# Window attention on one core: the right-hand columns of windows laid end to end over five blocks, a last block of three lines, and a start whose clearing moves to GpSimd

## The chip, the cores and the metric

The kernel runs on one core of one Trainium2 chip. The metric is the time of one execution in microseconds on the device. Times below are from three runs of the kernel before and from one profiled execution of it.

## The reference, cut to what matters

The image x is 511 x 511 with 192 channels in bf16 (73 x 73 windows of 7 x 7 pixels). A 3 x 3 depthwise convolution is added to it, the sum is normalised over its channels, each window does attention over its own 49 pixels with 4 heads of 48, and a projection is added back.

```python
xp = jnp.pad(x, ((0, 0), (1, 1), (1, 1), (0, 0)))
for i in range(3):
    for j in range(3):
        pe = pe + xp[:, i:i + H, j:j + W, :] * dw_pe[i, j][None, None, None, :]
x0 = x + pe
h = _layernorm(x0, axis=-1)
# h into windows of 7 x 7: 73 * 73 windows of 49 pixels
qkv = (hw @ w_qkv).reshape(-1, 49, 3, 4, 48)
attn = softmax(einsum('wnhd,wmhd->whnm', q, k) * 48 ** -0.5)
out = einsum('whnm,wmhd->wnhd', attn, v).reshape(-1, 49, 192) @ w_o
return x0 + out          # out back from windows to the image
```

## The kernel before

The 5329 windows are cut into 42 blocks of up to 128 windows; a window is a partition. `_blocks` gives each block as lines `(a, b, da, db, n, p)`: n windows from window (a, b) on, along a row (`db` = 1) or down a column (`da` = 1), on partitions from p. The first 64 windows of each of the 73 rows are lines of 64, two to a block. The nine columns on the right (columns 64 to 72) are lines of 64 down, rows 1 to 64. Blocks 0 to 35 are pairs of rows; block 36 is the last row and column 64; blocks 37 to 40 are pairs of columns; what is left in the right-hand corners, 81 windows, is block 41, nine lines of nine.

A block needs two loads. `load_xp` fetches XP, the patches for the convolution: 9 x 9 pixels on 81 partitions, then windows, then channels. One transfer brings, for one line, one of the nine pixel columns of the patch (9 patch rows x n windows x 192 channels); where a patch leaves the image, `clear` copies zeros. `load_x` fetches X, the pixels by windows (128 x 49 x 192); the same tile later takes the convolution, then the projection, and is stored from there. XP has one buffer, X has three. Loads and stores go through SP's queue in the order in which they are written; a few XP loads go through ScalarE's queue.

The main loop goes over 667 groups of 8 windows; a block has 16 groups (slots 0 to 15), the last one 11. While block b is in attention (`stage_A`: q and k, `stage_V`, `stage_B`: scores and their exponential, `stage_D`: the product with v, `stage_E`: transposition into HO), the same loop carries, spread over the slots by `part`,

- the projection of block b-1 in 13 pieces (`proj`): ScalarE copies a piece out of PSUM to pO and GpSimd adds it to X; with `direct` VectorE adds it from PSUM; then the stores of block b-1 in four chunks of rows (`store`),
- the convolution of block b+1: 192 matmuls, one per channel (`conv_mm`, L318), each ten of them added to X by VectorE (L324); then its layer norm: statistics (L329), `rstd` on GpSimd (L338, L339), the product h (L344), and its transposition into HO (`ln_tr`, L354 and L364),
- the loads of block b+2: XP once the convolution of block b+1 has read the one XP buffer, X once block b-1 is stored. For a block with 14 loads of X (two lines) an earlier path issues them as the stores of block b-1 leave.

Ahead of the loop block 0 is convolved and normalised with nothing beside it (`Next.prepare`), after some tiles have been cleared (HO, k, pt, v).

Of the kernel before, what the change touches and what calls it, by code (L numbers as in the profile page):

```python
# [32 lines left out]
WS, NH, C, DH, S = 7, 4, 192, 48, 49  # L33
BLK, CH, KP, KT = 128, 8, 81, 96
# [4 lines left out]
_HALF = 64  # L39


def _blocks(nwr, nwc):

    full, tall = min(_HALF, nwc), min(_HALF, nwr)
    top = min(1, nwr - tall)
    halves = [(a, 0, 0, 1, full) for a in range(nwr)]
    halves += [(top, b, 1, 0, tall) for b in range(full, nwc)]
    blocks = [[h + (64 * i,) for i, h in enumerate(halves[k : k + 2])] for k in range(0, len(halves), 2)]
    if nwc > full:
        cur, p = (blocks.pop(), 64) if len(halves) % 2 else ([], 0)  # L50
        for a in [*range(top), *range(top + tall, nwr)]:
            n = nwc - full
            if p + n > BLK:
                blocks.append(cur)
                cur, p = [], 0
            cur.append((a, full, 0, 1, n, p))
            p += n
        if cur:
            blocks.append(cur)
    return blocks  # L60


class _Kernel:
# [140 lines left out]
    def load_xp(self, b):  # L204

        nc, x, XP, XPr, W, NWR, NWC = self.nc, self.x, self.XP, self.XPr, self.W, self.NWR, self.NWC
        blocks, clear, dram = _blocks(NWR, NWC), self.clear, self.dram
        for a0, b0, da, db, n, p0 in blocks[b]:
            left = [0] if b0 == 0 else []
            right = [] if b0 + (n - 1) * db < NWC - 1 else list(range(n)) if da else [n - 1]  # L210
            if left and (b == 0 or any(ln[1] for bb in blocks[:b] for ln in bb)):
                yield clear(XPr[0], p0, n if da else 1)
            if right:
                yield clear(XPr[8], p0 + right[0], len(right))
            last = a0 + (n - 1) * da
            cuts = [0] + ([1] if da and a0 == 0 else []) + ([n - 1] if da and last == NWR - 1 else []) + [n]
            for i, j in zip(cuts, cuts[1:]):
                if j <= i:
                    continue
                top, bot = a0 + i * da == 0, a0 + (j - 1) * da == NWR - 1  # L220
                if top:
                    yield clear(XP[0:9], p0 + i, j - i)
                if bot:
                    yield clear(XP[KP - 9 : KP], p0 + i, j - i)
                pr0, pr1 = (1 if top else 0), (8 if bot else 9)
                for pc in range(9):
                    q, sh = (WS - 1, -1) if pc == 0 else (0, 1) if pc == 8 else (pc - 1, 0)
                    n0, n1 = i, j
                    if pc == 0 and left:
                        n0 = j if da else i + 1  # L230
                    if pc == 8 and right:
                        n1 = i if da else j - 1
                    if n1 <= n0:
                        continue
                    dims = [[W * C, pr1 - pr0], [WS * C * (W * da + db), n1 - n0], [1, C]]
                    dst = XPr[pc, pr0:pr1, p0 + n0 : p0 + n1, :]
                    src = dram(x, WS * (a0 + n0 * da) - 1 + pr0, WS * (b0 + n0 * db + sh) + q, dims)
                    q = nc.scalar if (len(blocks[b]) > 2 and pc % 3 == 2) or (b == 0 and pc % 2) else nc.sync
                    yield lambda q=q, dst=dst, src=src: q.dma_start(out=dst, in_=src)  # L239

    def strips(self, b, r0, r1):

        W = self.W
        for a0, b0, da, db, n, p0 in _blocks(self.NWR, self.NWC)[b]:
            yield slice(p0, p0 + n), (WS * a0 + r0, WS * b0, [[WS * C * (W * da + db), n], [W * C, r1 - r0], [1, WS * C]])

    def load_x(self, b):

        nc = self.nc
        short = len(_blocks(self.NWR, self.NWC)[b]) > 2  # L250
        for r0, r1 in [(0, WS)] if short else [(r, r + 1) for r in range(WS)]:
            for p, at in self.strips(b, r0, r1):
                dst = self.X[b % 3][p, r0 * WS : r1 * WS, :].rearrange("p (r q) c -> p r (q c)", q=WS)
                q = nc.sync
                yield lambda q=q, dst=dst, src=self.dram(self.x, *at): q.dma_start(out=dst, in_=src)


    def fast(self, ctx):
        nc, tc = self.nc, self.tc
# [12 lines left out]
        o_ = pool.tile([128, 2, 2, C], BF, name="o")  # L272
        pO = _Rot([pool.tile([128, 4, C], BF, name=f"pO{i}") for i in range(2)])
        r_ = pool.tile([128, 16], F32, name="rs")
        nc.vector.memset(HO[0][:], 0.0)
        nc.gpsimd.memset(HO[1][:], 0.0)
        nc.vector.memset(k_[:], 0.0)
        for t in [pt] + vv:
            nc.vector.memset(t[:], 1.0)

        x, out, W = self.x, self.out, self.W
        NWR, NWC = self.NWR, self.NWC
# [1 line left out]
        NB = len(blocks)  # L284
# [42 lines left out]
        def ln_stat(b, i):  # L327
            s = min(2 * i, S - 2)
            nc.vector.bn_stats(  # L329
                out=bnst[:, s : s + 2, :].rearrange("p a f -> p (a f)"),  # L330
                in_=self.X[b % 3][:, s : s + 2, :].rearrange("p s c -> p c s"),
            )

        def ln_rstd(r):

            t = slice(r * WS, (r + 1) * WS)
            e = nc.gpsimd
            e.tensor_scalar(out=rstd[:, t], in0=bnst[:, t, 2], scalar1=1.0 / C, scalar2=self.eps, op0=ALU.mult, op1=ALU.add)  # L338
            e.tensor_tensor(out=rstd[:, t], in0=rstd[:, t], in1=expo[:].to_broadcast([128, WS]), op=ALU.pow)  # L339

        def ln_norm(b, r, eng):
            t = slice(r * WS, (r + 1) * WS)
            h = self.X[2][:, t, :] if b == 0 else hr.next()
            eng.tensor_tensor(  # L344
                out=h[:, :, :], in0=self.X[b % 3][:, t, :], in1=rstd[:, t].unsqueeze(2).to_broadcast([128, WS, C]), op=ALU.mult
            )
            return h
# [151 lines left out]
        class Next:  # L499
# [15 lines left out]

            def prepare(n_):

                while n_.si < STATS:
                    ln_stat(n_.b, n_.si)
                    n_.si += 1  # L520
                for r in range(WS):
                    ln_rstd(r)
                    n_.ready.append((now[0], ln_norm(n_.b, r, nc.gpsimd if r < 2 else nc.vector)))
                    if r >= 2:
                        ln_tr(n_.b, n_.tr, n_.ready[n_.tr][1])
                        n_.tr += 1

# [24 lines left out]
            t()  # L552
        n.prepare()
        n.finish()
        sq = []
        nn = None

# [3 lines left out]
        for g in range(NG + LE + 1):  # L561
# [18 lines left out]
            def part(lo, hi, total, at=None):  # L580
                return min(total, max(0, int(((f if at is None else at) - lo) / (hi - lo) * total + 0.5)))

            pj = []
            even = b < NB and nslot >= 14
            if 1 <= b and ck >= (LE - 1 if even else LE):
                goal = 13 if b == NB else min(13, 3 * ck - 2) if even else part(0.10, 0.48, 13)
                while pdone < goal:
# [20 lines left out]
            def hook(share):  # L608

                nonlocal xpn, xln  # L610
                at = f0 + (f - f0) * share
                if n and n.conv.c == C:
                    n.stats(int(s_start + (s_goal - s_start) * share))
                while sq and sq[0][0] <= g + share:
                    _, bb, k = sq.pop(0)
                    store(bb, k)
                    stored[bb] = k + 1
                    freed[k] = g + share
                if even and 1 <= b and len(xl) == 2 * WS:
                    while xln < len(xl) and freed.get(xln // 4, NG) + 0.9 <= g + share:  # L620
                        xl[xln]()
                        xln += 1
                if n is None or n.conv.c == C:
                    goal = part(0.38 + d, 0.96 if many else 0.58 + 0.5 * d, len(xp), at)
                    while xpn < goal:
                        xp[xpn]()
                        xpn += 1
                    if b < 1 or stored.get(b - 1, 0) == len(CHUNKS):
                        goal = part(0.5, 0.7, len(xl), at)
                        while xln < goal:  # L630
                            xl[xln]()
                            xln += 1
# [5 lines left out]
            def project(groups_):  # L638
                nonlocal sdone
                for s0 in groups_:  # L640
                    proj(b - 1, s0, b == NB and s0 % 8 == 0)
                    while sdone < len(CHUNKS) and CHUNKS[sdone][1] * WS <= min(S, s0 + 4):
                        sq.append((g + 0.9, b - 1, sdone))
                        sdone += 1
# [286 lines left out]
```

## Time and profile before

| what | value |
|---|---|
| runs of the kernel | 3611.0, 3615.5 and 3599.74 us, median 3611.0 us |
| the profiled execution | 3608.29 us, of which the span of instructions is 3606.6 us |
| mean granted clock of TensorE | 0.986 |
| busy: PE, PEld, DVE, ACT, POOL | 92%, 82%, 69%, 78%, 57% |

The span is what the trace shows; 1.7 us lie around it. The busy shares are means over the whole span, in which one block takes some 82 us, so what a stage costs has to be read in stretches of a block. A stretch is best cut where the first matmul of a convolution stands, since the convolution of a block and the load of XP for the one after it follow each other in one buffer.

### The profile page before, as it was taken

Reading aid. Unit: us, or ns where it says so; the run is one execution under the profiler, and the core shown is the slowest. Engines: PE = TensorE matmul, PEld = TensorE weight load, DVE = VectorE, ACT = ScalarE, POOL = GpSimd, SP = SyncE. Lnnn points to the kernel's source line nnn. Section 1 sums busy time; section 2 is a strip of 40 time slices with the busy share of each in tenths; the row PEclk is TensorE's granted clock in tenths of the full one; section 3 lists DMA queues with packets and bytes.
Section 4 is the critical chain, followed back from the end, with each engine's and each line's share of the span. In section 5 each row is a group of like instructions: output and inputs, shape, how many; then the busy total and the mean of one; then the engine's idle time right before and its main releaser. Section 6 shows DMA issues by size and latency. Waiting matters only on the chain.

```text
span 3606.6 us, 170088 instructions
## 1 busy us (share of the span) xinstructions
PE 3330.4 (92%) x77393; PEld 2941.1 (82%) x77393; DVE 2504.5 (69%) x4236; ACT 2804.7 (78%) x3512; POOL 2063.1 (57%) x1425
## 2 busy tenths in 40 slices
PE   4999999999999999999999999999999999999687
PEld 3888888888888888888888888888888888888575
DVE  6767667777776667777777766777777766666563
ACT  1788888888888888888888888888888877777575
POOL 4356655666555566566655566656665555555453
PEclk9999999999999999999999999999999998999898
DMA  6344444444434444444444444444444444444311
GB/s 145 74 101 108 115 117 116 117 113 113 103 101 101 106 112 116 119 118 114 115 104 101 101 107 112 116 117 118 114 117 103 101 101 101 101 101 105 67 32 46
DMA packets 529123, 377.39 MB, mean 105 GB/s; under 512 B 453595, under 2 KB 453787, under 8 KB 528393
## 3 DMA queue, kind: packets, MB, share of 16 engines
q1 hardware_dynamic: 521440, 363.75, 40.8%
q8 instruction: 607, 9.95, 1.2%
q10 hardware_dynamic: 6953, 2.69, 0.4%
q14 instruction: 123, 1.01, 0.1%
HBM read 265.31 MB, written 100.27 MB: 101 GB/s over the span
## 4 chain that ended last, share of the span: by engine, by line
PE 63%; DVE 15%; ACT 9%; issue 4%; POOL 3%; SPq 3%; DMA 3%; ACTq 0%; POOLq 0%; DVEq 0%
PE ps L378 19%; PE ps L473 11%; PE psc L318 9%; PE ps L394 9%; PE ps L461 7%; DVE bnst L329 6%; DVE o L447 4%; PE psc L354 4%; ACT pO L484 4%; ACT v L402 3%; SPq L239 3%; PE ps L437 2%; POOL h L344 2%; DVE HO L462 2%; PE ps L416 2%
## 5 line engine op out<-in xcount | busy, mean ns | idle before, releaser
L488 POOL TENSOR_TENSOR X<-X,pO 128x768 bf16<-128x768 bf16 (+1 forms) x539 | 845.8, 1573 | 1097.9 <-ACT pO L484 1095.5
L378 PE MATMUL ps<-HO,Wqk 96*128 96x196 bf16 (+1 forms) x7680 | 1318.4, 283 | 89.3 <-ACT pO L484 49.0
L318 PEld LDWEIGHTS <-XP 81*128 81x128 bf16 x8064 | 1014.4, 175 | 105.3 <-issue 95.5
L318 PE MATMUL psc<-T,XP 81*128 81x49 bf16 x8064 | 1036.0, 205 | 48.6 <-DMA XP<-in_x_dram 34.6
L378 PEld LDWEIGHTS <-Wqk 96*128 96x128 bf16 x7680 | 753.7, 104 | 150.6 <-issue 22.5
L324 DVE TENSOR_TENSOR X<-psc,X 128x490 bf16<-128x490 f32 x840 | 539.1, 645 | 448.9 <-PE psc L318 445.9
L386 ACT CAST k<-ps 128x784 bf16<-128x784 f32 x667 | 542.0, 813 | 243.3 <-PE ps L378 220.2
L344 POOL TENSOR_TENSOR h<-X,rstd 128x1344 bf16<-128x1344 bf16 x287 | 697.9, 2432 | 22.5
L386 ACT CAST q<-ps 128x784 bf16<-128x784 f32 x667 | 542.2, 813 | 187.2 <-PE ps L378 146.5
L394 PE MATMUL ps<-Wv,HO 96*128 96x192 bf16 x5336 | 646.6, 245 | 22.8 <-ACT q L386 19.7
L447 DVE TENSOR_TENSOR o<-ps,rs 128x768 bf16<-128x768 f32 x667 | 638.8, 958 | 23.3
L394 PEld LDWEIGHTS <-HO 96*128 96x128 bf16 x5336 | 515.0, 104 | 106.6 <-issue 69.7
L424 ACT ACTIVATE pt<-ps 128x784 bf16<-128x784 f32 x667 | 550.1, 825 | 55.8 <-PE ps L416 40.5
L402 ACT CAST v<-ps 128x768 bf16<-128x768 f32 x667 | 536.3, 804 | 69.3 <-PE ps L394 58.6
L329 DVE BATCH_NORM_STATS2 bnst<-X 128x6 f32<-128x384 bf16 x1050 | 533.9, 547 | 4.2
L462 DVE COPY HO<-ps 96x784 bf16<-96x784 bf16 x667 | 380.0, 570 | 209.5 <-PE ps L461 207.4
L484 ACT CAST pO<-ps 128x768 bf16<-128x768 f32 x498 | 397.7, 799 | 145.8 <-PE ps L473 127.5
L473 PE MATMUL ps<-Wo,HO 96*128 96x192 bf16 x4116 | 491.3, 262 | 1.4 <-DVE HO L462 0.7
L461 PEld LDWEIGHTS <-o 128*96 128x96 bf16 x5336 | 364.8, 125 | 109.3 <-DVE o L447 78.5
L339 POOL TENSOR_TENSOR rstd<-rstd,expo 128x7 f32<-128x7 f32 x294 | 439.2, 1494 | 24.5
L461 PE MATMUL ps<-ident,o 128*96 128x128 bf16 x5336 | 421.4, 222 | 24.8 <-DVE o L447 22.6
L473 PEld LDWEIGHTS <-HO 96*128 96x128 bf16 x4116 | 436.8, 186 | 1.9 <-DVE HO L462 0.9
(55 smaller groups left out, 2604.9 us busy)
## 6 DMA issues: line engine op xcount, KB each, us to landing
XP<-in_x_dram SPq DMA_DIRECT2D x644, 216.0 KB
X<-in_x_dram SPq DMA_DIRECT2D x574, 168.0 KB
out_dram<-X SPq DMA_DIRECT2D x246, 336.0 KB
XP<-in_x_dram SPq DMA_DIRECT2D x71, 212.6 KB
out_dram<-X SPq DMA_DIRECT2D x82, 168.0 KB
XP<-in_x_dram SPq DMA_DIRECT2D x12, 192.0 KB
X<-in_x_dram SPq DMA_DIRECT2D x9, 165.4 KB
XP<-in_x_dram SPq DMA_DIRECT2D x42, 30.4 KB
```

Of the source, the lines that this page charges most:

```text
L318: mm(cv.ps[:, (c % 10) * S : (c % 10 + 1) * S], lhsT=XP[0:KP, :, c], rhs=T[0:KP, c, :], start=True, stop=True)
L329: nc.vector.bn_stats(out=bnst[:, s : s + 2, :].rearrange("p a f -> p (a f)"), in_=self.X[b % 3][:, s : s + 2, :].rearrange("p s c -> p c s"),)
L344: eng.tensor_tensor(out=h[:, :, :], in0=self.X[b % 3][:, t, :], in1=rstd[:, t].unsqueeze(2).to_broadcast([128, WS, C]), op=ALU.mult)
L378: mm(ps[:, ab * 512 + i * m * S : ab * 512 + (i + 1) * m * S], lhsT=self.Wqk[kt][0:KT, which * 2 + ab, :], rhs=HO[b % 2][0:KT, kt, ck * CH ...
L386: nc.scalar.copy(out=dst[:, :, 0:TOK], in_=two_bank(ps, TOK))
L394: mm(ps[:, col : col + C], lhsT=HO[b % 2][0:KT, kt, w : w + 2, :].rearrange("p w s -> p (w s)"), rhs=self.Wv[kt][0:KT, :], start=(kt == 0) ...
L402: eng(out=v_[:].rearrange("p (b j) h e -> p b (j h) e", b=2)[:, :, :, 0:DH], in_=two_bank(ps, 2 * C).rearrange("p b (g d) -> p b g d", d=DH),)
L424: nc.scalar.activation(out=pt[:, 0 : 16 * S].rearrange("p (b n) -> p b n", b=2), in_=two_bank(ps, 8 * S), func=ACTF.Exp, scale=SCALE)
L447: nc.vector.tensor_tensor(out=o_[:].rearrange("p b q (h d) -> p b (q h) d", d=DH), in0=ov[:, :, :, 0:DH], in1=r_[:].rearrange("p (b g) -> ...
L461: mm(ev, lhsT=o_[:, sl, Q, kt * KT : (kt + 1) * KT], rhs=ident[:], start=True, stop=True, is_transpose=True)
L473: mm(ps[:, col : col + C], lhsT=HO[b % 2][0:KT, kt, :, s0 + i], rhs=self.Wo[kt][0:KT, :], start=(kt == 0), stop=(kt == 1))
L488: nc.gpsimd.tensor_tensor(out=xv, in0=xv, in1=o[:, 0:n, :], op=ALU.add)
```

## The change

The right-hand columns: `_blocks` now takes the nine columns with rows 1 to 71 and lays them end to end, cutting wherever a block is full. 639 windows fill blocks 36 to 40 (2, 3, 3, 3 and 2 lines, the last with 127 windows). Block 41 is the last row (64 windows) and the nine corner windows of the first and of the last row: three lines, 82 windows. The number of blocks and groups stays.

With that: `load_x` fetches X of a line with all seven pixel rows in one transfer wherever a block has columns; `strips` cuts a line of n windows at the last multiple of 16, for loads and stores alike, so a line of 71 becomes 64 and 7; ScalarE's queue issues XP loads for block 0 alone; XP loads of blocks of three lines are written by 0.62 of a block instead of 0.96.

The start: HO[0], k, pt and v are cleared on GpSimd instead of VectorE, and HO[1] on GpSimd after block 0 is prepared; `prepare` takes the rows one by one (statistics, rstd, h of the row before on VectorE or GpSimd in turn, transposition), where all 25 statistics came first.

The last block: the projection of block 40 stands in slots 1 to 5 of block 41 (1, 3, 3, 3, 3 pieces) instead of slots 2 to 5 (6, 3, 3, 1), and every second piece of it is added by VectorE.

```diff
-    full, tall = min(_HALF, nwc), min(_HALF, nwr)
-    top = min(1, nwr - tall)
+    full = min(_HALF, nwc)
+    n = nwc - full
     halves = [(a, 0, 0, 1, full) for a in range(nwr)]
-    halves += [(top, b, 1, 0, tall) for b in range(full, nwc)]
...
+    if n:
+        last, p = (blocks.pop(), _HALF) if nwr % 2 else ([], 0)
+        cur, q = [], 0
+        for b in range(full, nwc):
+            a = 1
+            while a < nwr - 1:
+                m = min(nwr - 1 - a, BLK - q)
+                cur.append((a, b, 1, 0, m, q))
+                a, q = a + m, q + m
+                if q == BLK:
+                    blocks.append(cur)
+                    cur, q = [], 0
         if cur:
             blocks.append(cur)
+        blocks.append(last + [(a, full, 0, 1, n, p + i * n) for i, a in enumerate((0, nwr - 1))])
...
-                    q = nc.scalar if (len(blocks[b]) > 2 and pc % 3 == 2) or (b == 0 and pc % 2) else nc.sync
+                    q = nc.scalar if b == 0 and pc % 2 else nc.sync
...
+            for i, m in ((0, n - n % 16), (n - n % 16, n % 16)):
+                if m:
+                    at = (WS * (a0 + i * da) + r0, WS * (b0 + i * db), [[WS * C * (W * da + db), m], [W * C, r1 - r0], [1, WS * C]])
+                    yield slice(p0 + i, p0 + i + m), at
...
-        short = len(_blocks(self.NWR, self.NWC)[b]) > 2
+        lines = _blocks(self.NWR, self.NWC)[b]
+        short = len(lines) > 2 or any(ln[2] for ln in lines)
...
-        nc.vector.memset(HO[0][:], 0.0)
-        nc.gpsimd.memset(HO[1][:], 0.0)
-        nc.vector.memset(k_[:], 0.0)
+        nc.gpsimd.memset(HO[0][:], 0.0)
+        nc.gpsimd.memset(k_[:], 0.0)
         for t in [pt] + vv:
-            nc.vector.memset(t[:], 1.0)
+            nc.gpsimd.memset(t[:], 1.0)
...
-                while n_.si < STATS:
-                    ln_stat(n_.b, n_.si)
-                    n_.si += 1
-                for r in range(WS):
-                    ln_rstd(r)
-                    n_.ready.append((now[0], ln_norm(n_.b, r, nc.gpsimd if r < 2 else nc.vector)))
-                    if r >= 2:
+                for r in range(WS + 1):
+                    if r < WS:
+                        while n_.si < min(STATS, ((r + 1) * WS + 1) // 2):
+                            ln_stat(n_.b, n_.si)
+                            n_.si += 1
+                        ln_rstd(r)
+                    if r:
+                        n_.ready.append((now[0], ln_norm(n_.b, r - 1, nc.vector if r % 2 else nc.gpsimd)))
+                    if r > 1:
...
         n.finish()
+        nc.gpsimd.memset(HO[1][:], 0.0)
...
-            even = b < NB and nslot >= 14
+            even = b < NB and nslot >= 8
...
-                    goal = part(0.38 + d, 0.96 if many else 0.58 + 0.5 * d, len(xp), at)
+                    goal = part(0.38 + d, 0.62 if many else 0.58 + 0.5 * d, len(xp), at)
...
-                    proj(b - 1, s0, b == NB and s0 % 8 == 0)
+                    proj(b - 1, s0, b >= NB - 1 and s0 % 8 == 0)
```

The first place is SP's queue while block 35 is in attention: the stores of block 34 and the loads of block 37, which is made of columns. Before (`out_dram` is the output, X_74 the X buffer, `in_x_dram` the image; shapes are partitions first):

```order
L303 DMA out_dram<-X_74 64x2x1344 x4
L255 DMA X_74<-in_x_dram 64x1344 x8
L303 DMA out_dram<-X_74 64x2x1344 x2
L303 DMA out_dram<-X_74 64x1344 x2
L255 DMA X_74<-in_x_dram 64x1344 x6
L239 DMA XP<-in_x_dram 9x64x192 x18
```

The same place in the change:

```order
L310 DMA out_dram<-X_74 64x2x1344 x6
L310 DMA out_dram<-X_74 64x1344 x2
L243 DMA XP<-in_x_dram 9x14x192 x9
L243 DMA XP<-in_x_dram 9x71x192 x5
L263 DMA X_74<-in_x_dram 14x7x1344
L243 DMA XP<-in_x_dram 9x71x192 x4
L263 DMA X_74<-in_x_dram 64x7x1344
L243 DMA XP<-in_x_dram 9x43x192 x7
L263 DMA X_74<-in_x_dram 7x7x1344
L243 DMA XP<-in_x_dram 9x43x192 x2
L263 DMA X_74<-in_x_dram 32x7x1344
L263 DMA X_74<-in_x_dram 11x7x1344
```

X was fetched ahead of XP in 14 transfers; it is now fetched in five, which stand among the 27 of XP and behind them. In every block of columns it is so.

The second place is SP's queue while block 39 is in attention, with the loads of block 41. Before, this is the beginning of 74 transfers on SP (27 more are on ScalarE's queue):

```order
L200 DMA XP<-T 9x192
L200 DMA XP<-T 9x9x192
L239 DMA XP<-in_x_dram 8x9x192 x6
L200 DMA XP<-T 9x192
L239 DMA XP<-in_x_dram 9x9x192 x2
L255 DMA X_75<-in_x_dram 9x7x1344
L239 DMA XP<-in_x_dram 9x9x192 x2
L255 DMA X_75<-in_x_dram 9x7x1344
```

The same place in the change, from the first transfer (`XP<-T` is `clear`) to the clears ahead of the third line:

```order
L204 DMA XP<-T 9x192
L204 DMA XP<-T 9x64x192
L243 DMA XP<-in_x_dram 8x63x192
L243 DMA XP<-in_x_dram 8x64x192 x8
L204 DMA XP<-T 9x192
L204 DMA XP<-T 9x9x192
L243 DMA XP<-in_x_dram 8x9x192 x6
L263 DMA X_75<-in_x_dram 64x7x1344
L243 DMA XP<-in_x_dram 8x9x192 x2
L243 DMA XP<-in_x_dram 8x8x192
L204 DMA XP<-T 9x192
L204 DMA XP<-T 9x9x192
```

All of block 41's patches are now three lines: nine transfers of a row of 64 windows, eighteen small ones and six clears, where there were 81 small ones and eleven clears.

The third place is VectorE at the start, from the branch into the fast path on. Before, the rows of clearing and the first two additions of the convolution of block 0:

```order
L267 MEMSET expo 128x1
L275 MEMSET HO_260 128x8192
L277 MEMSET k 128x408
L279 MEMSET pt 128x800
L279 MEMSET v_268 128x784
L279 MEMSET v_269 128x784
L324 TENSOR_TENSOR X_73<-psc_67,X_73 128x49x10
L324 TENSOR_TENSOR X_73<-psc_68,X_73 128x49x10
```

In the change the additions come at once, and behind the last of them the statistics, h (X_75) and the transposed rows (HO) alternate (the last rows of that stretch):

```order
L275 MEMSET expo 128x1
L331 TENSOR_TENSOR X_73<-psc_67,X_73 128x49x10
...
L336 BN_STATS bnst<-X_73 128x6 x7
L351 TENSOR_TENSOR X_75<-X_73,rstd 128x1344
L336 BN_STATS bnst<-X_73 128x6 x4
L371 COPY HO_260<-psc_67 96x128x7
L351 TENSOR_TENSOR X_75<-X_73,rstd 128x1344
```

The five clears are gone from VectorE's queue, and four products h stand between the statistics instead of five behind them.

## Rows read from the trace of the kernel before

**Rows 1.** The page: span, engines, and the granted clock in 40 slices.

```profile
span 3606.6 us, 170088 instructions
...
PE 3330.4 (92%) x77393; PEld 2941.1 (82%) x77393; DVE 2504.5 (69%) x4236; ACT 2804.7 (78%) x3512; POOL 2063.1 (57%) x1425
...
PEclk9999999999999999999999999999999998999898
```

**Rows 2.** Busy time by stretch, cut where each next convolution starts (blocks 33 to 39).

```profile
2793.50:2875.20 81.70, 78.25 (x1854) 69.21 (x1853) 58.81 (x101) 66.95 (x85) 49.08 (x34) 1.00 0.44 111
2875.20:2962.80 87.60, 82.13 (x1930) 71.68 (x1929) 60.51 (x103) 69.67 (x88) 49.11 (x34) 0.98 0.43 103
2962.80:3048.80 86.00, 79.72 (x1861) 70.33 (x1862) 59.68 (x101) 67.55 (x85) 48.98 (x34) 0.98 0.44 106
3048.80:3139.40 90.60, 84.62 (x1861) 75.15 (x1862) 59.16 (x100) 67.25 (x84) 49.04 (x34) 0.91 0.42 100
3139.40:3224.70 85.30, 78.09 (x1860) 69.00 (x1861) 59.18 (x100) 67.11 (x84) 49.00 (x34) 1.00 0.44 106
3224.70:3312.70 88.00, 81.82 (x1861) 72.72 (x1861) 59.10 (x100) 67.26 (x84) 48.98 (x34) 0.94 0.43 103
3312.70:3433.90 121.20, 81.00 (x1861) 71.14 (x1862) 59.20 (x100) 67.68 (x84) 49.06 (x34) 0.85 0.28 56
```

**Rows 3.** The convolution's matmuls alone (L318), from first to last, blocks 34 to 38.

```profile
2875.20:2920.00 44.80, 24.46 (x192) 23.90 (x191) 1.00 0.32 81
2962.80:3008.30 45.50, 24.57 (x192) 24.07 (x192) 1.00 0.39 101
3048.80:3100.20 51.40, 28.25 (x192) 26.41 (x192) 0.83 0.33 86
3139.40:3184.90 45.50, 24.59 (x192) 24.07 (x192) 1.00 0.39 101
3224.70:3273.80 49.10, 27.01 (x192) 25.59 (x192) 0.90 0.36 91
```

**Rows 4.** Waits of PE from 3359 to 3440 us: sum, times, longest.

```profile
PE psc L318 <- DMA XP<-in_x_dram: 33.0, 1, 33.0
```

**Rows 5.** Transfers into XP, 3359 to 3440 us: ns of an issue (min/median/max), first and last.

```profile
L239 SPq DMA_DIRECT2D XP<-in_x_dram x54: 676/763/803, 3364.0 to 3431.6; - x54
L239 ACTq DMA_DIRECT2D XP<-in_x_dram x27: 686/783/1441, 3359.8 to 3396.7; - x27
L200 SPq DMA_DIRECT2D XP<-T x11: 757/777/857, 3359.6 to 3427.1; - x11
```

**Rows 6.** SP's queue in order of time: loads of a block of rows, then of columns.

```profile
2838.27 3.10 SPq L239 DMA_DIRECT2D XP<-in_x_dram  x3
2841.49 5.16 SPq L255 DMA_DIRECT2D X<-in_x_dram  x6
2846.69 21.04 SPq L239 DMA_DIRECT2D XP<-in_x_dram  x15
...
3100.68 34.55 SPq L239 DMA_DIRECT2D XP<-in_x_dram  x18
```

**Rows 7.** The start: VectorE's timeline, waits for X of L324, GpSimd's rstd.

```profile
36.12 6.88 DVE L275 MEMSET HO<- 128x8192 uint32 x1 [1.68 <-issue]
...
45.84 1.18 DVE L324 TENSOR_TENSOR X<-psc,X 128x490 bf16<-128x490 f32 x2
...
L324 DVEq EVENT_SEMAPHORE  x4: 49/50/50, 40.4 to 42.0; - x4
...
L339 POOL TENSOR_TENSOR rstd<-rstd,expo 128x7 f32<-128x7 f32 x7 | 15.1, 2155 | 0.6
```

**Rows 8.** The end: one stretch of block 41, last additions on GpSimd, last stores.

```profile
3524.20:3559.80 35.60, 32.10 (x626) 25.94 (x626) 10.82 (x19) 27.71 (x38) 19.88 (x13) 0.95 0.28 70
...
3589.68 4.88 POOL L488 TENSOR_TENSOR X<-X,pO 128x768 bf16<-128x768 bf16 x3
...
3587.75 16.39 SPq L303 DMA_DIRECT2D out_dram<-X  x36
```

More of the change, by code (lines that the diff above doesn't have):

```diff
@@ L42, in _blocks @@
 def _blocks(nwr, nwc):
-    full, tall = min(_HALF, nwc), min(_HALF, nwr)
-    top = min(1, nwr - tall)
+    full = min(_HALF, nwc)
+    n = nwc - full
+    assert 2 * n <= _HALF
     halves = [(a, 0, 0, 1, full) for a in range(nwr)]
-    halves += [(top, b, 1, 0, tall) for b in range(full, nwc)]
     blocks = [[h + (64 * i,) for i, h in enumerate(halves[k : k + 2])] for k in range(0, len(halves), 2)]
[L49 to L57, printed above, removed]
+    if n:
[10 more added lines that the diff above has]
+                    cur, q = [], 0
         if cur:
             blocks.append(cur)
+        blocks.append(last + [(a, full, 0, 1, n, p + i * n) for i, a in enumerate((0, nwr - 1))])
     return blocks
@@ L244, in strips @@
         for a0, b0, da, db, n, p0 in _blocks(self.NWR, self.NWC)[b]:
-            yield slice(p0, p0 + n), (WS * a0 + r0, WS * b0, [[WS * C * (W * da + db), n], [W * C, r1 - r0], [1, WS * C]])
+            for i, m in ((0, n - n % 16), (n - n % 16, n % 16)):
+                if m:
+                    at = (WS * (a0 + i * da) + r0, WS * (b0 + i * db), [[WS * C * (W * da + db), m], [W * C, r1 - r0], [1, WS * C]])
+                    yield slice(p0 + i, p0 + i + m), at
     def load_x(self, b):
         nc = self.nc
-        short = len(_blocks(self.NWR, self.NWC)[b]) > 2
+        lines = _blocks(self.NWR, self.NWC)[b]
+        short = len(lines) > 2 or any(ln[2] for ln in lines)
         for r0, r1 in [(0, WS)] if short else [(r, r + 1) for r in range(WS)]:
```

## Prediction, written before the changed kernel ran

> **What bounds the kernel now.** The page first [rows 1]: TensorE (PE) is busy 92% of a span of 3606.6 us, and its granted clock is full (2.4 GHz) until the last sixth of the slices (a 9 is 0.9 or more). So for most of the span PE sets the pace, and nothing that only takes work off another engine moves the end. Then the stretches cut at each convolution's start [rows 2]. A block of rows takes 81.7 us. Block 34, during which the first columns are loaded, takes 87.6, and blocks 35 to 38 take 86.0, 90.6, 85.3 and 88.0; block 39 takes 121.2 with PE busy for 81.0 of it. Three places are thus worth looking at: blocks 34 to 38, block 39, and the two ends, where no block overlaps another.
>
> Block 39 is plain: PE waits once, 33.0 us, for XP [rows 4]. The convolution of block 41 is waiting for its patches. Behind that wait stand 92 transfers into XP, 65 of them on SP at some 0.76 us each, issued from 3359.6 to 3431.6 us [rows 5]. Issuing is the bound, 72 us of it, since one transfer brings nine windows only. With PE idle the clock falls to half, 1.2 GHz, and the stretch has 0.85 of the full one [rows 2].
>
> Blocks 34 to 38 are subtler. XP has one buffer, so a block is a loop: the convolution (45 us at full clock, up to 51.4 at a mean of 0.83 [rows 3]), then the loads, then the next convolution. A block of rows has its 18 XP loads and six X loads issued in 3.10 + 5.16 + 21.04 us, 1.40 us for an XP load [rows 6]. For columns 18 XP loads alone take 34.55 us, 1.92 each [rows 6]: the same bytes, spread over more of the image. In block 36 the first is issued at 3100.68 us, 0.5 us behind the convolution, the last is through at 3135.23, and the next convolution starts at 3139.4, 4.2 us later [rows 2, 3, 6]. From the first issue that is 38.7 us. So the loop takes 45.5 + 0.5 + 38.7 = 84.7 us at full clock, just what PE itself needs for such a block (85.3 [rows 2]). PE waits there hardly at all, but nothing is left either: each microsecond that the loads grow by is paid.
>
> **The change, part by part.**
>
> *Start.* VectorE (DVE) spends 36.12 to 45.8 us on clears before its first addition, and PE waits for that [rows 7]. Without them the addition waits for X alone, whose last semaphore is there at 42.0 us [rows 7]: 45.8 - 42.0 = 3.8 us gained (2.8 to 5.4: the four waits ended between 40.4 and 42.0, and one landing may lie later by 1 us). The clears move to GpSimd, which has no work until the first rstd, well past 60 us; HO[1] then lies on it beside the first slots of block 0, where it has none either. If that cover were gone, its 13 us would stand on the path. Preparing block 0 row by row starts rstd and the products h among the statistics, but rstd stays a chain of seven on GpSimd, 15.1 us at a mean of 2.16 [rows 7], and GpSimd now has three products h instead of two. I count 1.2 us gained (0 to 3). Together **-5** (-2 to -8).
>
> *Columns end to end.* The windows in XP are as many as before, so I take 38.7 us from first issue to restart, and add what is new among the loads.
> X: it left ahead of XP, now it stands among it. The six X loads of a row block put 29.3 - 18 x 1.40 = 4.1 us between its XP loads [rows 6], 0.7 us for 64 window rows of pixels. Written ahead of the last XP load are, in blocks 34 to 38, 64, 85, 92, 106 and 56 windows of seven pixel rows, which is 7.0, 9.3, 10.1, 11.6 and 6.1 such loads: 4.9 + 6.5 + 7.0 + 8.1 + 4.3 = 30.8 us. That is the upper bound; nothing is the lower, if X runs in the gaps that XP leaves (a column's XP moves at 1.40/1.92 of the rate of a row's).
> Short pieces: nine XP loads of 14 windows cost 9 x 0.76 us to issue [rows 5], against 14/64 x 1.92 = 0.42 each by volume, and no queue stands before them: 3 us in block 35. The other pieces are long enough, or come when the queue is full.
> Block 34 had half a block of columns and goes to a whole one. With convolutions of 44.8 us in block 34 and 47.9 (mean of the other four [rows 3]) after it, the loops are 44.8 + 0.5 + 38.7 + 4.9 = 88.9, then 97 (with the short pieces), 94, 95 and 91: 466 us against 437.5 [rows 2], +29. With X hidden it is -2. I take two thirds of the X term, since XP's queue is not full all the time: **+20** (-2 to +40, the upper end with a longer half-clock stretch behind each wait, as the 5.9 us between 51.4 and 45.5 in block 36 [rows 3]).
> The stores of these blocks are cut too, 16 to 24 instead of 8. They are issued while the convolution runs, ahead of the loads; if they came late they would push XP by some 0.6 us each.
>
> *Block 41's patches.* Nine loads of the last row (9 x 1.40 = 12.6 us), eighteen small ones and six clears (24 x 0.77 = 18.5), three of X (2): 33 us, then 4.2 to the restart. The loop is 47.9 + 0.5 + 33 + 4.2 = 85.6 against a PE bound of 85.3, so block 39 takes about 86 where it took 121.2: **-35** (-33 to -36.5).
> The Trainium skill has a rule against this ("DMA: Bandwidth & Descriptors", Rules for kernel authors): gather small transfers into large ones, since under 64 KB mostly overhead is paid, some 2 us each (its fit is for the GpSimd path). By that the 18 small loads would take 36 us instead of 14, an estimate from the page, and block 39 would end near 108. The trace differs: 54 such loads were issued at a median of 0.76 us [rows 5], without a gap of that size.
>
> *Last block.* In slots 0 to 5, 35.6 us, PE is busy for 32.1 [rows 8]; six projections in one slot had to pass through GpSimd. Spread evenly, half of them on DVE, most of the 3.5 us idle goes: -3 (0 to -4). At the very end GpSimd's last addition is through at 3594.6 us, but the 36 stores, issued over 16.39 us, end at 3604.1 [rows 8]. Twelve stores instead: the last three can leave behind that addition, at some 0.45 us each, so 3596: -8 (-6 to -9). Together **-11**.
>
> Blocks 1 to 33 and block 40 carry the same instructions and stay. **Sum**: -5 + 20 - 35 - 11 = -31 us on the profiled 3608.3, that is 3577. The median of the three runs is 2.7 us higher, the lowest 8.6 lower; I leave 3577.
>
> **The rivals.** Changes below 0.5% (18 us) are about what three runs of this kernel can't tell from none; the edge on the fast side is 3593.
> A, the columns cost nothing: X hides behind XP, which for columns leaves gaps. The sum is -53, 3555. For it: 1.92 us against 1.40, so the engines of the transfers aren't full; against it: in the row block X did stop XP.
> B, the columns cost the whole of their bound and some clock: +35 to +60, so 3592 to 3617, no change. For it: PE has no slack in these loops, and each wait brought half clock behind it [rows 2].
> C, slower. The next convolution waits for X, not XP: part of X is written behind the last XP load, and DVE's first addition needs all of it; PSUM holds twenty channels, then PE stands. All 128 windows are 14 loads, 14 x 0.7 = 9.8 us, and with the 4.2 to landing each of five transitions costs 14, together 70: 3608 - 51 + 70 = 3627. It decides from 14 us a transition on. Against it: what stands behind the last XP load is 22 to 71 windows, 1.7 to 5.5 us, and PE has twenty channels of work first.
> D, block 41's loads don't shrink, because something else in SP's queue (stores of three lines, clears that wait) holds them: half of the 35 remains, 3595. For it: SP runs in order; against it: 24 small transfers at 0.77 us are already counted. It would be seen as a wait for XP before the convolution of block 41. By the Trainium skill's rule on small transfers (the section above) the 35 would be 13 and the time 3599, an estimate from the page.
>
> **How the numbers follow.** The forecast (columns +5 to +35) holds 0.55, its own range 3562 to 3592; A 0.18; B with D 0.20; C 0.07. Faster: forecast and A, 0.73; same 0.20; slower 0.07. The range takes in A at its middle and the lower half of B: 3552 to 3604.
>
> **What would show it.** Right: in the trace after, the first addition of block 0 near 42 us; no wait for XP of over 5 us in block 39, which takes 84 to 90; waits of PE for XP of 3 to 11 us at the ends of blocks 35 to 38, which take 89 to 97; SP's last store within 3 us of GpSimd's last addition. Wrong: if blocks 34 to 38 take 86 as before, X was hidden (A); if they take over 100, it is C, and VectorE's wait for X tells it.

## The result, and the profile after

The change made the kernel slower: 3642.27 us median (3636.97 to 3642.72, four runs) against 3607.09 us (3599.74 to 3615.5, four runs) of the kernel before beside it, a ratio of 1.009 (95% interval 1.0075 to 1.0104). The profiled execution took 3642.7 us.

The page of the changed kernel, the lines that answer to [rows 1]:

```profile
span 3641.0 us, 170009 instructions
...
PE 3341.7 (92%) x77393; PEld 2951.3 (81%) x77393; DVE 2507.1 (69%) x4243; ACT 2799.5 (77%) x3505; POOL 2070.9 (57%) x1424
...
PEclk9999999999999999999999999999999998989899
```

The busy times hardly moved (PE +11 us). What grew is idle time. The granted clock is below 0.9 in three slices near the end, as before, and its mean is 0.982 where it was 0.986. The stretches say where. Busy time by stretch, cut at the starts of the convolutions as in [rows 2] (columns: stretch, its length, then PE, PEld, DVE, ACT and POOL busy, granted clock, DMA share, GB/s); blocks 33 to 39:

```profile
2793.06:2875.37 82.31, 78.86 (x1854) 69.65 (x1853) 58.78 (x101) 66.94 (x85) 49.08 (x34) 1.00 0.44 110
2875.37:2972.78 97.41, 85.27 (x1929) 74.34 (x1928) 60.68 (x103) 69.77 (x88) 49.09 (x34) 0.93 0.45 91
2972.78:3077.22 104.44, 80.12 (x1860) 70.68 (x1861) 59.73 (x101) 67.53 (x85) 48.99 (x34) 0.92 0.43 87
3077.22:3176.65 99.43, 83.06 (x1861) 73.19 (x1861) 59.49 (x100) 67.30 (x84) 49.01 (x34) 0.91 0.46 91
3176.65:3282.35 105.70, 85.18 (x1860) 75.79 (x1861) 59.18 (x100) 67.17 (x84) 49.05 (x34) 0.86 0.43 87
3282.35:3373.90 91.55, 80.01 (x1861) 70.80 (x1861) 59.09 (x100) 67.11 (x84) 49.04 (x34) 0.97 0.44 92
3373.90:3477.76 103.86, 86.45 (x1860) 76.92 (x1861) 59.20 (x100) 67.02 (x84) 49.03 (x34) 0.86 0.31 72
```

Until block 34 the sum is nil: its stretch starts at 2875.37 us, where it was 2875.20. Blocks 34 to 38 then take 498.5 us instead of 437.5, **+61.0**, where the prediction had +20. Block 39 takes 103.9 instead of 121.2, **-17.3**, where it had -35. From the start of block 41's convolution to its first exponential the two are alike (89.5 and 90.3 us, -0.8), and the last block with its tail takes 73.7 instead of 82.4, **-8.7**, where it had -11. With the +0.2 ahead of block 34 that is the +34.4 us of the spans.

In blocks 34 to 39 PE waits for loads. Waits of PE from 2875 to 3480 us (sum, times, longest), then those of VectorE, then SP's own:

```profile
PE psc L325 <- DMA X<-in_x_dram: 30.6, 3, 13.4
PE psc L325 <- DMA XP<-in_x_dram: 20.1, 2, 15.2
PE ps L423 <- issue: 11.6, 5, 4.7
...
PE psc L325 <- DVE X L331: 5.7, 4, 2.5
```

```profile
DVE X L331 <- DMA X<-in_x_dram: 7.5, 3, 3.4
```

```profile
SPq L204 <- DMA XP<-T: 10.8, 3, 5.8
```

Read the first two rows together. The instruction that waits is the first matmul of a convolution, which reads XP and not X. Loads of XP and of X take turns on the same eight semaphores, and the wait has the name of the load that last raised one of those awaited. Who really needs X is VectorE's addition (L331), and it waited 7.5 us in all. The semaphore updates in the trace settle it: the last patch loads for the convolutions that start at 3077.22, 3176.65 and 3282.35 us were issued at 3067.93, 3165.41 and 3272.79 and had landed at 3076.88, 3176.30 and 3282.11, just before, while loads of X were still landing. So in the changed kernel it is the patches that come late. SP's queue shows them in block 35, with X between the pieces (start, length, transfers):

```profile
3021.99 13.98 SPq L243 DMA_DIRECT2D XP<-in_x_dram  x14
3036.08 2.29 SPq L263 DMA_DIRECT2D X<-in_x_dram  x1
3038.41 9.02 SPq L243 DMA_DIRECT2D XP<-in_x_dram  x4
3047.47 3.20 SPq L263 DMA_DIRECT2D X<-in_x_dram  x1
3050.72 15.24 SPq L243 DMA_DIRECT2D XP<-in_x_dram  x7
3066.00 0.77 SPq L263 DMA_DIRECT2D X<-in_x_dram  x1
3067.11 1.59 SPq L243 DMA_DIRECT2D XP<-in_x_dram  x2
3068.75 1.50 SPq L263 DMA_DIRECT2D X<-in_x_dram  x2
```

From the first XP load to the last the queue needs 46.7 us, and the last one lands 9 us after its issue. PE stands idle for 15.2 us at its end: the convolution of block 37 could have started at 3062 us and starts at 3077.22.

### The profile page after: what moved, and what is told of

The parts are those of the page before. It is cut to its first block, busy times and chain, and to the rows that moved or that the text cites. A ratio compares the mean times of both kernels' runs of the same rounds, so it can differ in the third digit from the quotient of the medians.

```text
span 3641.0 us, 170009 instructions
## 1 busy us (share of the span) xinstructions
PE 3341.7 (92%) x77393; PEld 2951.3 (81%) x77393; DVE 2507.1 (69%) x4243; ACT 2799.5 (77%) x3505; POOL 2070.9 (57%) x1424
## 4 chain that ended last, share of the span: by engine, by line
PE 61%; DVE 17%; ACT 8%; issue 4%; SPq 4%; POOL 3%; DMA 3%; ACTq 0%; POOLq 0%; DVEq 0%
PE ps L385 18%; PE ps L480 11%; PE psc L325 9%; PE ps L401 8%; PE ps L468 7%; DVE bnst L336 6%; DVE o L454 5%; PE psc L361 4%; ACT pO L491 4%; SPq L243 3%; ACT v L409 3%; DMA X<-in_x_dram 2%; PE ps L444 2%; DVE HO L469 2%; POOL h L351 2%
## 5 line engine op out<-in xcount | busy, mean ns | idle before, releaser
L495 POOL TENSOR_TENSOR X<-X,pO 128x768 bf16<-128x768 bf16 (+1 forms) x532 | 835.7, 1574 | 1144.9 <-ACT pO L491 1140.5
L325 PEld LDWEIGHTS <-XP 81*128 81x128 bf16 x8064 | 1017.8, 175 | 117.3 <-issue 88.9
L325 PE MATMUL psc<-T,XP 81*128 81x49 bf16 x8064 | 1041.5, 206 | 66.3 <-DMA X<-in_x_dram 34.0
L331 DVE TENSOR_TENSOR X<-psc,X 128x490 bf16<-128x490 f32 x840 | 538.4, 645 | 464.7 <-PE psc L325 446.4
```

Of the source, the lines that this page charges most:

```text
L325: mm(cv.ps[:, (c % 10) * S : (c % 10 + 1) * S], lhsT=XP[0:KP, :, c], rhs=T[0:KP, c, :], start=True, stop=True)
L495: nc.gpsimd.tensor_tensor(out=xv, in0=xv, in1=o[:, 0:n, :], op=ALU.add)
```

## The experiments

The theory, from these rows: **X is what makes the columns dear**, because it now stands among and behind XP in SP's queue. The rival: the lines laid end to end, with their 27 XP loads where there were 18 and their cut stores, slow the loads by themselves. Expectations count a block from its first exponential to that of the next (blocks 34 to 38: 435.3 us before, 500.1 after); the text uses the stretches above (437.5 and 498.5). In the stretches of blocks 34 to 38 I separate the convolutions, from the first to the last matmul of each, from the rest, in which XP is loaded. A third column tells how much of the rest had passed when the last patch load landed, by the semaphore updates in the traces (a load of nine patch rows makes nine as it lands); what is left of the rest is PE's slack, time in which the patches were there and PE was still busy with attention.

| kernel | convolutions | the rest | of it, until the last patch landed | sum, us |
|---|---|---|---|---|
| before | 236.5 | 201.0 | 194.3 | 437.5 |
| the change | 244.9 | 253.7 | 248.6 | 498.5 |
| without X (e2) | 232.6 | 207.7 | 197.0 | 440.3 |
| X behind XP (e8) | 288.0 | 212.1 | 207.7 | 500.1 |
| X for four of seven rows (e10) | 236.1 | 228.0 | 225.0 | 464.2 |
| X of 64 windows row by row (e6) | 251.9 | 250.9 | 250.2 | 502.7 |
| X ahead of XP (e1) | 239.3 | 218.0 | 211.6 | 457.3 |
| the same, clears of block 41 in a row (e9) | 233.1 | 218.7 | 213.7 | 451.7 |
| the same, X of block 41 ahead too (e7) | 234.1 | 216.9 | 213.0 | 451.1 |
| before, with X whole (e3) | 244.2 | 238.2 | 227.8 | 482.4 |

In e4 and e5 below, which leave these blocks as in the kernel before, the sums are 435.9 and 435.3: some 2 us is the spread of one trace.

**e1, X ahead of XP again.** X of blocks 36 to 40 goes in four chunks of pixel rows, 16 to 24 transfers a block, as the stores of block b-1 leave:

```diff
-        short = len(lines) > 2 or any(ln[2] for ln in lines)
-        for r0, r1 in [(0, WS)] if short else [(r, r + 1) for r in range(WS)]:
+        if any(ln[2] for ln in lines):
+            rows = [(0, 2), (2, 4), (4, 6), (6, 7)]
+        else:
+            rows = [(0, WS)] if len(lines) > 2 else [(r, r + 1) for r in range(WS)]
+        for r0, r1 in rows:
...
-                if even and 1 <= b and len(xl) == 2 * WS:
-                    while xln < len(xl) and freed.get(xln // 4, NG) + 0.9 <= g + share:
+                if even and 1 <= b and len(xl) > 3:
+                    per = 4 if len(xl) == 2 * WS else len(xl) // 4
+                    while xln < len(xl) and freed.get(xln // per, NG) + 0.9 <= g + share:
```

> The changed kernel, but X of blocks 36 to 40 is fetched in four transfers of rows per piece, each as soon as the stores of block b-1 free those rows, so all of it stands ahead of XP in SP's queue. Theory X (the loads of X that stand among and behind those of XP are what made blocks 34 to 38 long): their XP loads are issued in 35 to 40 us instead of 42 to 48, the waits for X at their ends go, blocks 34 to 38 come down from 500 us together to 440 to 455, the kernel to about 3590. Theory L, the rival (the lines end to end themselves: 27 shorter XP loads a block, other addresses): XP takes as long as in the changed kernel, the time stays above 3625.

Measured: 3588.85 us (3586.75 to 3596.5), a ratio to before of 0.9928 (0.9901 to 0.9956). With X moved, and cut into chunks for that, the change is faster than the kernel before. Blocks 34 to 38 give back 41 of the 61 us, and 47 in e9 and e7, where their loads stand as here.

**e2, no X at all** in blocks 36 to 40:

```diff
+        if any(ln[2] for ln in lines):
+            return
```

> The changed kernel without any load of X for blocks 36 to 40 (left out: the convolution is added to what the buffer held). Theory X: nothing stands among XP, blocks 34 to 38 take 85 to 90 each, only block 35 (nine XP loads of 14 windows) up to 92; time at or below 3595. Theory L: the trains of XP stay at 42 us and more, blocks at 95 and more, time above 3625.

Measured: 3582.13 us, one run. Blocks 34 to 38 come to 440.3 us, 2.8 above the kernel before, and X costs 58.2 us where the change puts it. Lines end to end, with 27 loads instead of 18 and the cut stores, do not slow the loads by themselves: the last patch has landed after 197.0 us, where it took 194.3 in the kernel before, 198.2 in e4 and 195.0 in e5. As the cause of the 61 us the rival falls. But the kernel before has an early X, and this run has none. Put early on the new lines (e1, e9, e7), X costs 11 to 17 us, and the five blocks stay some 14 to 22 us above before. So 41 to 47 of the 61 us are X's place in the queue.

**e3, the kernel before with X of its column blocks whole:**

```diff
-        short = len(_blocks(self.NWR, self.NWC)[b]) > 2
+        short = len(_blocks(self.NWR, self.NWC)[b]) > 2 or any(ln[2] for ln in _blocks(self.NWR, self.NWC)[b])
```

> The kernel before, changed in one thing: X of the blocks with columns (36 to 40) is fetched with all seven pixel rows in one transfer for each line, two a block, which by the unchanged rules then stand among the XP loads. Theory X: 5 to 10 us more for each of five blocks, 3630 to 3650. Theory L: within 8 us of before.

Measured: 3659.73 us (3650.11 to 3668.73), ratio 1.0127 (1.0091 to 1.0164). This one line alone, on the old geometry, makes the blocks 44.9 us longer (9 a block; the whole is above its range).

**e6, the 64-window transfers of X as seven of one pixel row each**, at the same place in the queue:

```diff
...
+                if r1 - r0 == WS and p.stop - p.start == 64:
+                    def each(dst=dst, p=p, at=at):
+                        for r in range(WS):
+                            dims = [at[2][0], [at[2][1][0], 1], at[2][2]]
+                            nc.sync.dma_start(out=dst[:, r : r + 1, :], in_=self.dram(self.x, at[0] + r, at[1], dims))
+                    yield each
+                    continue
...
```

> The changed kernel, but each X load of 64 windows x 7 rows is cut into seven of one row at the same place in SP's queue. If the shape of the one large transfer (448 descriptors of 2688 bytes, window by window) is what stops XP for 8 to 10 us, the seven cost some 5 us as in a block of rows: 3610 to 3625. If the place alone counts (any X among XP), within 8 us of the changed kernel, or slower by SP's seven issues instead of one (3640 to 3655).

Measured: 3649.48 us (3643.61 to 3653.39), ratio 1.0094 (1.0064 to 1.0125), and 502.7 us in the five blocks. Cutting the large transfers, which carry half of the windows of such a block, brings nothing; the place counts.

**e8, X behind the last XP load** instead of among the loads:

```diff
-                    if b < 1 or stored.get(b - 1, 0) == len(CHUNKS):
+                    if (b < 1 or stored.get(b - 1, 0) == len(CHUNKS)) and (early or xpn == len(xp)):
```

> The change, with X of the blocks of columns written behind the last XP load instead of among the loads. Theory: X among XP stretches the XP loads (42 to 52 us from the first to the last in the change, 34 to 40 without X), so the XP loads come back to 34 to 40 us here; but then the whole of X, 128 windows, stands behind them, and VectorE's first addition waits for it. If X costs the same 10 us for 64 windows there, each transition waits 10 to 15 us for X after PE's first twenty channels, blocks 34 to 38 stay at 95 to 105 us and sum to 480 to 510. Rival: it is only the mixing of the two in the queues that is slow, and X alone goes at 0.7 us for 64 window rows, 9.8 us in all; then PE waits 5 to 9 us a transition and the five blocks sum to 455 to 475.

Measured: 3657.22 us, one run. SP's queue in block 35, and VectorE's waits from 2875 to 3500 us:

```profile
3026.26 38.44 SPq L243 DMA_DIRECT2D XP<-in_x_dram  x27
3064.81 4.62 SPq L263 DMA_DIRECT2D X<-in_x_dram  x5
```

```profile
DVE X L331 <- DMA X<-in_x_dram: 63.2, 6, 14.8
```

The 27 XP loads are back to 38.4 us from 46.7. But now VectorE waits for X in every transition, up to 14.8 us, PE soon stands too, and each convolution that waits takes 55 to 64 us instead of 47 to 54 in the change, at a lower granted clock. Two of them alone (L325, from first to last matmul):

```profile
2971.15:3026.23 55.08, 27.00 (x192) 25.55 (x192) 0.88 0.29 64
3070.82:3134.45 63.63, 27.97 (x192) 26.14 (x192) 0.80 0.37 71
```

In the table nearly the whole bill has moved from "the rest" to "convolutions", and the sum is the same. That is how rival C looks, and it shows that the change itself was not C.

**e10, four of seven pixel rows of X**, as a price by amount:

```diff
-        for r0, r1 in [(0, WS)] if short else [(r, r + 1) for r in range(WS)]:
+        for r0, r1 in [(0, 4 if any(ln[2] for ln in lines) else WS)] if short else [(r, r + 1) for r in range(WS)]:
```

> The change, but X of the blocks of columns is fetched for four of the seven pixel rows only, in the same transfers at the same places (three rows of X of each column block are left out, and of the work nothing else). Theory: X among and behind XP is paid by what it brings, so of the 63 us that blocks 34 to 38 lose to X (500.1 in the change, 436.8 without X) four sevenths stay: 473 us, 465 to 481. Rival, on which the prediction took two thirds of the X term: XP leaves gaps in the queue that hide part of X, so the first rows are free and only the rest is paid; then four sevenths cost clearly less than their share, 437 to 460.

Measured: 3603.87 us, one run. Four sevenths of X cost 464.2 - 440.3 = 23.9 of the 58.2 us, 41% for 57%. By exponentials it is 462.6, between the two bands. The landings tell why. Until the last patch has landed, four rows of X add 225.0 - 197.0 = 28.0 us and seven add 51.6, so four sevenths are 54%: in the queue X is paid by what it brings, and XP leaves no gaps that hide it. What hides the first part is PE: without X the patches are there 10.7 us (over the five blocks) before PE wants them, in e10 3.0.

**e9 and e7, block 41.** e9 is e1 with the six clears of XP written together, ahead of the 27 loads (a second pass over the lines issues the loads). e7 is e9 with X of block 41 in chunks ahead of XP as well:

```diff
-        if any(ln[2] for ln in lines):
+        if len(lines) > 2 or any(ln[2] for ln in lines):
             rows = [(0, 2), (2, 4), (4, 6), (6, 7)]
```

> As the first run of this study (X of blocks 36 to 40 ahead of XP), with only the six clears of block 41 moved ahead of its loads; X of block 41 stays among XP as in the change. Theory: the clears' waits for each other (2.2 + 2.95 + 5.8 = 11 us in the change) pass beside the convolution, so block 39 goes from 97.7 to about 90 us; what is left over 86 is X of block 41, which is written among and behind XP. Rival: X alone is what holds block 39; then it stays at 96 to 99 us here.

> The change, with X of blocks 36 to 40 ahead of XP in chunks of rows (as in the first run of this study), and in block 41 two more edits: the six clears of XP are written together ahead of its 27 loads, and X of block 41 also goes ahead in chunks of rows. Theory: in the change block 39 took 100.3 us because three clears each waited for an overlapping one to land (11 us of waits in SP's queue) and because X came behind XP (a wait of 9.45 us). Without both the loop of block 39 is the forecast one, so block 39 goes from 97.7 us in the first run to 84 to 90, and the whole to 3575 to 3582. Rival: the clears cost the same in a row, since they overlap each other wherever they stand, and the small loads behind them are held by the landing of the last; then block 39 stays above 94 and the whole above 3585.

Measured: e9 3587.01 us (3583.98 to 3589.86), ratio 0.9939 (0.9918 to 0.9959); e7 3577.32 us (3572.98 to 3578.78), ratio 0.9906 (0.9889 to 0.9923). SP's queue for block 41 in the changed kernel, from the first clear on:

```profile
3429.06 3.96 SPq L204 DMA_DIRECT2D XP<-T  x2
3433.07 14.38 SPq L243 DMA_DIRECT2D XP<-in_x_dram  x9
3447.50 5.07 SPq L204 DMA_DIRECT2D XP<-T  x2
3452.61 4.33 SPq L243 DMA_DIRECT2D XP<-in_x_dram  x6
...
3459.87 7.44 SPq L204 DMA_DIRECT2D XP<-T  x2
3467.36 4.33 SPq L243 DMA_DIRECT2D XP<-in_x_dram  x6
```

Then the same queue in e7, and the stretch of block 39 in e9 and in e7:

```profile
3375.45 9.19 SPq L204 DMA_DIRECT2D XP<-T  x6
3384.69 24.80 SPq L250 DMA_DIRECT2D XP<-in_x_dram  x27
```

```profile
3329.61:3418.32 88.71, 80.48 (x1860) 71.32 (x1861) 59.10 (x100) 67.09 (x84) 49.06 (x34) 0.97 0.34 76
```

```profile
3327.66:3413.86 86.20, 80.14 (x1861) 71.09 (x1861) 59.10 (x100) 67.05 (x84) 49.07 (x34) 0.98 0.33 79
```

Two clears take 1.6 us to issue; they stand here for 3.96, 5.07 and 7.44, since each line's second clear overlaps the first and waits for it to land (10.8 us in three waits). Written in a row, the six take 9.19 us. They do not pass beside the convolution, as was expected: XP is still read there, and in e7 the first is issued 0.9 us behind the convolution's end at 3374.56. Block 39 goes from 95.1 us in e1 to 88.7 in e9, and with X ahead to 86.2.

**e4, the start alone**, on the kernel before (the start's lines of the diff):

> The kernel before with the start of the change alone (clears on GpSimd, block 0 prepared row by row). Theory: the first exponential of block 1 came at 176.25 us before and at 173.31 with the change, 2.9 us earlier, and that is the start's share; here it comes at 173 to 174.5, and the rest of the run stays as before. Rival: those 2.9 us are spread of the start of a run; then it comes at 176 or later here.

Measured: 3609.08 us, one run; the first exponential of block 1 at 172.97 us, 3.3 earlier than before. So the start is earlier by the change's own edits, by too little for the times of the whole to show.

**e5, the last block alone**, on the kernel before:

```diff
-            even = b < NB and nslot >= 14
+            even = b < NB and nslot >= 8
...
-                    proj(b - 1, s0, b == NB and s0 % 8 == 0)
+                    proj(b - 1, s0, b >= NB - 1 and s0 % 8 == 0)
```

> The kernel before with the last block's edit alone (projection of block 40 in slots 1 to 5, every second piece added by VectorE); the nine lines of block 41 and their 36 stores stay. Theory: from the start of block 41 to its last exponential took 50.7 us before and 48.1 with the change, and that is the projection's share, so here it takes 48 to 49 us, while the 31.7 us from the last exponential to the end stay at 31 to 32, since those became 25.6 by the twelve stores in place of 36. Rival: the spread projection also shortens the end, because GpSimd comes to its last additions earlier; then the end takes 29 us or less here.

Measured: 3603.48 us, one run. From the first to the last exponential of block 41 48.1 us (50.7 before), and from there to the end 31.7 as before. So the spread projection is worth some 2.6 us (e4 and e3, with the old projection, have 49.3 and 52.1), and the rest of the last block's gain belongs to the stores.

## Why the prediction was wrong

**The step that failed is the X term** of "Columns end to end", with a mechanism that was named and a size that was too small. It took 0.7 us for 64 window rows from the X loads of a block of rows [rows 6], 30.8 us for all that is written ahead of the last XP load, and two thirds of that, since XP's queue was thought to have gaps. The landings give what it is: with X among the loads the last patches are 248.6 - 197.0 = 51.6 us later, 51.6 / 44 = 1.17 us for 64 window rows if what stands behind the last XP load adds nothing, and e10 shows no gap that hides it. PE's slack takes 5.6 of it, so "the rest" grows by 253.7 - 207.7 = 46.0 us. Even the row gave more than 0.7: its six X loads stand for 5.16 us in the queue, 0.86 each, and 0.7 came from counting all 18 XP loads at 1.40 us where the first three took 1.03. And the sum took too little for what such waits do to the next convolution. It counted 44.8 + 4 x 47.9 = 236.4 us of convolutions and kept a longer half-clock stretch for the upper end of its range; with X among the loads they take 244.9, without X 232.6, so 12.3 us are X's, and the granted clock is lower in them. Two convolutions behind long waits (L325, as in [rows 3]) show it, the second with 28.7 us of PE busy where 24.6 do at full clock:

```profile
3077.22:3127.09 49.87, 26.80 (x192) 25.37 (x192) 0.92 0.23 56
3176.65:3230.30 53.65, 28.73 (x192) 26.67 (x192) 0.83 0.23 52
```

Together 58.2 us, where 20.5 stood. The step around it held as a sum: without X the five blocks came 2.8 us above before, where -2 had been forecast, the 3 us for the short pieces in it. "Nothing is left" held for two of the five loops: without X, three had the last patch 1.2 to 5.9 us before PE wanted it. In the kernel before, X of these blocks left early, as the stores freed the buffer; whether it cost anything there no run shows, but giving up that path was the expensive line of the change, 44.9 us on the old lines (e3) and 41 to 47 on the new ones (e1, e9, e7).

**Rivals.** It is B's mechanism (the whole bound and some clock), beyond its bound and at +61.0 just past its upper end; the time is past B's 3617 since block 41 gave less as well. Not C: two of five blocks took over 100 us, which the prediction's sign would have put down to C, but VectorE waited for X only 7.5 us. A is refuted.

**Block 41's patches, -35: half came.** 33 us of issuing were right but for the clears: the queue took 45.9 us from 3429.06, of which 10.8 were waits of clears. That is the place of rival D, clears that wait. From the convolution's end the loads took 103.9 - 55.1 = 48.7 us against the 37.7 forecast, 11.0 more. The other part is the convolution itself, 55.1 us at a granted clock of 0.80 where 47.9 had been counted: it comes out of the columns' waits (45.5 to 46.9 us in e1, e9 and e7, where those are short). The two make up the 18.3 us by which the block exceeds the forecast 85.6. With both gone and X of block 41 ahead (e7), block 39 takes 86.2 us; forecast was 86. The Trainium skill's rule on small transfers ("DMA: Bandwidth & Descriptors", Rules for kernel authors), with the 2 us that the page fits for one transfer of the GpSimd path, would have had some 36 us for the 18 small loads, an estimate; six were issued in 4.33 us, 0.72 each, so the measurement decides against it here.

**The start, -5**: the first addition is at 42.28 us (forecast 42.0, before 45.84). The row-by-row preparation brought nothing more that shows; the first exponential of block 1 came 2.9 us earlier, in e4 3.3. But blocks 1 to 33, forecast to stay, gave it back: from the first exponential of block 1 to that of block 34 it was 2707.1 to 2708.9 us in the three traces with the old start (before, e3, e5) and 2710.1 to 2714.4 in the nine with the new one. Why was not found. GpSimd's clears are over well ahead of its first rstd at 61.3 us:

```profile
34.72 13.76 POOL L283 MEMSET HO<- 128x16384 bf16 x1 [25.80 <-DVE expo L275]
48.42 0.78 POOL L284 MEMSET k<- 128x816 bf16 x1
49.14 0.76 POOL L286 MEMSET pt<- 128x800 bf16 x1
49.85 1.44 POOL L286 MEMSET v<- 128x784 bf16 x2
```

**The last block, -11**: -8.7. The projection gave 2.6 of 3. The end gave 6.1 of 8: GpSimd's last addition ends at 3634.6 us and the span 6.4 later, where 12.0 had been between them [rows 1, 8]. The last of the stores is through at 3638.0, 3.4 behind the addition, where 1.4 had been forecast. GpSimd's and SP's last rows (SP's takes in eight stores of block 40 besides the twelve):

```profile
3626.42 8.14 POOL L495 TENSOR_TENSOR X<-X,pO 128x768 bf16<-128x768 bf16 x5 [0.37 <-ACT pO L491]
```

```profile
3594.21 43.80 SPq L310 DMA_DIRECT2D out_dram<-X  x20
```

**What stays open.** Even ahead of XP, X costs 10 us in "the rest" (218.0 against 207.7 in e2). Most of it is X's own issuing: in e1 the first XP load starts 1.9, 3.5, 1.8 and 0.9 us behind the convolution in blocks 35 to 38, 8.0 us over the five blocks where it is 0.2 in e2, as here behind the convolution that ends at 3014.72 us:

```profile
3010.16 6.38 SPq L266 DMA_DIRECT2D X<-in_x_dram  x10
3016.63 37.19 SPq L243 DMA_DIRECT2D XP<-in_x_dram  x27
```

PE's waits in L423 with no releaser in the profile, 11.6 us in five, are not explained.

## What to carry to other kernels

When a change takes work out of one queue, ask what the queue now carries between the transfers that the next stage waits for: here one load that had left early cost 41 to 47 us more, over five blocks, as soon as it stood among the critical ones, and as much behind them. Price such a load in the stretch where it will stand, and where no row shows that, let the bound go past the nearest row, with the clock behind the wait in the sum. And read a wait's name by the instruction that waits: the first matmul reads XP, whatever load the wait is named after.

## What was not expected of the hardware

The mean busy share of the DMA engines did not tell how fast they were. Over blocks 34 to 38 it was 0.44 at 89 GB/s in the change, and 0.43 at 99 GB/s in e1, which moves the same bytes to within 2% (45.26 MB for 44.59) in a different order; in e2, without X, 0.33 at 75. Busy time for each byte was thus some 13% higher with X among XP (0.44 x 498.5 / 44.59 against 0.43 x 457.3 / 45.26; 11 to 16% by the rounding of the shares):

```profile
2875.37:3373.90 498.53, 413.64 (x9370) 364.81 (x9368) 298.16 (x503) 338.89 (x424) 245.17 (x170) 0.92 0.44 89
```

```profile
2876.62:3333.91 457.29, 410.73 (x9369) 362.52 (x9368) 297.33 (x503) 338.12 (x424) 245.11 (x170) 0.94 0.43 99
```

The second is e1. These means take in the convolutions, with a share of 0.23 in the two shown above. From the end of a convolution to the start of the next the share was 0.60, 0.69 and 0.64 in blocks 35 to 37 of the change, at 114 to 126 GB/s, and PE stood there for loads that were still under way. A DMA share well below 1 thus did not mean that the loads could come sooner; whether single engines were full is not shown.
